# Sink-and-window attention with a highway layer on one core: later block loads in small rings, and the gate's bias split into eight pieces

## The chip, the cores and the metric

One core of a Trainium2 chip. The metric is device time in microseconds. The engines of the core run in order, each from its own queue, and wait for each other by semaphores: PE (matmul and weight load), DVE and ACT (elementwise work), POOL (GpSimd; it also issues the loads of q, k and v), and SP (it issues the stores).

## The reference

Attention with 4 batches, 8 heads, 768 positions and head size 64, in which each query sees the first 4 positions of its sequence (the sink) and the last 128; then a highway layer on the 3072 x 512 result.

```python
def _attn_ref(q, k, v, n_sink, window):
    scores = scale * np.matmul(q, k.transpose(0, 1, 3, 2))
    is_sink = pos[None, :] < int(n_sink)
    rel = pos[:, None] - pos[None, :]
    in_window = (rel >= 0) & (rel < int(window))
    scores = np.where(is_sink | in_window, scores, -1e9)
    a = np.exp(scores - np.max(scores, axis=-1, keepdims=True))
    a = a / (np.sum(a, axis=-1, keepdims=True) + 1e-09)
    return np.matmul(a, v)

def _moe_ref(x, w_h, w_t, b_t):
    H = np.maximum(x @ w_h, 0.0)
    T = 1.0 / (1.0 + np.exp(-(x @ w_t + b_t)))
    return T * H + (1.0 - T) * x
```

All inputs and the output are float32. The kernel computes in float16 with float32 accumulation, and writes the sigmoid as a tanh of half the argument.

## The kernel before, in words

The 3072 rows are 24 blocks of 128 queries, six to a batch. The keys and values of block n are loaded shifted by 64 positions (`chunk_parts`), so that a query block needs three pieces: its own shifted chunk n, half of chunk n+1, and half of chunk n-1. A shifted chunk at a batch border comes as two loads of 64 rows.

Each block passes through these steps, named as in the kernel's order string, with the engine and the line:

- `load_q`, `load_k`, `load_v` (POOL, L107, L114, L121): loads from DRAM that also convert to float16. q and k go to rotating buffers of a pool, v to the tiles of `v_ring`, in which a column of twos stands beside each head's 64 values for the row sums.
- `S` (PE): transposes of the q and k of a later block (L318; block n hosts those of block n+2), scores with the own chunk (`pe_SA`, L371) and with the two half chunks (`pe_SB`, L384; 64 x 64 matmuls on all four quarters of the array).
- `xx`, or `x0_` and `x1_` in early blocks (ACT, L398 and L393): the exponential, to the tile `e`. `tt`, or `tq` and `tk` (ACT, L330 and L323): the transposed q and k out of PSUM.
- `mm`, or `m0_` and `m1_` (DVE, L404): the mask. `sk` and `es` (PE L353, ACT L360): scores of the sinks and their exponential, for two blocks at a time after the first batch.
- `A` (PE): the values. `pe_AB` (L429) has 16 matmuls of 66 columns for the two half chunks, on the two quarters of the array that lead from one half of the rows to the other half of the columns; then eight full matmuls (L448) and two for the sinks (L454), all into the one PSUM tile `av`.
- `xh` (DVE, L462 and L467): division by the row sums. `X` (PE, L481) transposes the result into a spare part of `av`, and `xT` (ACT, or `xTV` on DVE, L486) copies it out; only then can the next `A` write `av`.
- `Mh` and `Mt` (PE, L509 and L497): the two products of the highway layer, into two PSUM banks `m`, which are dealt out by the string `M_BANKS` to these, to the sink scores and to the bias. The bias of `Mt` is a matmul of a row of ones by `bt16`: in blocks 0 to 7 one full matmul of 512 columns (L494), from block 9's `A` on (for the block before it) a pair of 64 x 64 matmuls of 512 columns in `pe_bias` (L437).
- `u` (ACT, L502), `U`, `d`, `e`, `o` (DVE, L521, L515, L526, L531): tanh, plus one, relu(H) minus x, product, sum; then the store by SP (L533).

The order on every engine is written out by hand in `ORDER`; a step issues its instructions in that order, so POOL's queue has the loads where the steps `A` stand: `do_A(n)` issues the loads of q of block n+8 and of k and v of chunk n+9. POOL itself does not wait for `A`; it waits only where a buffer is still read or the loads in flight hold it. At the first key chunk of batches 1 to 3, `new_T` puts the sinks' keys and values into block-diagonal tiles on POOL (`fill_ks`, L342, and `sink_v`, L181). The loads of the first blocks (q to 7, k and v to 8) are written out ahead of the loop.

Of the kernel before, what the change touches and what calls it, by code (L numbers as in the profile page):

```python
# [8 lines left out]
FP16 = mybir.dt.float16  # L9
# [11 lines left out]
def kernel(  # L21
# [18 lines left out]
    nc = tc.nc  # L40
    P = 128

    B, H, S, D = q.shape
# [8 lines left out]
    NSC = S // P  # L52
    assert NSC % 2 == 0
    NB = NT // P
# [4 lines left out]
    AHEAD = 8  # L59

    const = ctx.enter_context(tc.tile_pool(name="const", bufs=1))
    sd_pool = ctx.enter_context(tc.tile_pool(name="p_sd", bufs=AHEAD + 2))
    qkT_pool = ctx.enter_context(tc.tile_pool(name="p_qkT", bufs=7))
    tt_pool = ctx.enter_context(tc.tile_pool(name="p_tt", bufs=5))
    e_pool = ctx.enter_context(tc.tile_pool(name="p_e", bufs=3))
# [20 lines left out]

    ctx.callback(close_s)
    HP = P // 2
    B0 = 9
    M0 = 9  # L90
    NV = AHEAD + 5
    NS4 = H * NSINK
    KW = NHP * P + 32
    EW = P + HP
    v_ring = [const.tile([P, VW], FP16, tag=f"v{i}", name=f"v{i}") for i in range(NV)]
    q_sd, k_sd = {}, {}

    def chunk_parts(n):
        b, c = divmod(n, NSC)
        if c:  # L100
            return [(slice(0, P), b, c * P - HP)]
        return ([(slice(0, HP), b - 1, S - HP)] if b else []) + ([(slice(HP, P), b, 0)] if b < B else [])

    def load_q(n):
        b, c = divmod(n, NSC)
        qsd = sd_pool.tile([P, H, D], FP16, tag="qsd", name="qsd")
        nc.gpsimd.dma_start(out=qsd, in_=q[b, :, c * P:(c + 1) * P, :].transpose([1, 0, 2]))  # L107
        q_sd[n] = qsd

    def load_k(n):  # L110
        ksd = sd_pool.tile([P, H, D], FP16, tag="ksd", name="ksd")
        for rows, b, s0 in chunk_parts(n):
            nr = rows.stop - rows.start
            nc.gpsimd.dma_start(out=ksd[rows], in_=k[b, :, s0:s0 + nr, :].transpose([1, 0, 2]))  # L114
        k_sd[n] = ksd

    def load_v(n):
        vt = v_ring[n % NV][:, 0:H * 65].rearrange("p (h e) -> p h e", e=65)
        for rows, b, s0 in chunk_parts(n):
            nr = rows.stop - rows.start  # L120
            nc.gpsimd.dma_start(out=vt[rows, :, 0:D], in_=v[b, :, s0:s0 + nr, :].transpose([1, 0, 2]))  # L121
# [14 lines left out]
    bt32 = const.tile([P, DM], FP32, tag="bt32")  # L136
    bt16 = const.tile([P, DM], FP16, tag="bt16")
    ones_row = const.tile([P, P], FP16, tag="ones_row")
    ones2 = const.tile([P, P], FP16, tag="ones2")
    kf_first = const.tile([P, H, D], FP32, tag="kf0", name="kf0")  # L140
    ident32 = const.tile([P, P], FP32, tag="ident32")
    ident2 = const.tile([P, P], FP16, tag="ident2")
# [45 lines left out]
    with tc.manual_schedule(engines={ENG.Pool, ENG.SP}):  # L188
# [7 lines left out]
        for b in range(B):  # L196
            nc.sync.dma_start(out=vs_dn[b], in_=v[b, :, 0:NSINK, :])
        nc.gpsimd.affine_select(
            out=ident, in_=ident, compare_op=ALU.is_equal, fill=0.0,
# [14 lines left out]
            out=bm, in_=bm, compare_op=ALU.is_ge, fill=0.0,  # L214
            base=0, pattern=[[-NSINK, H]], channel_multiplier=1)
        nc.gpsimd.affine_select(
            out=bm, in_=bm, compare_op=ALU.is_ge, fill=0.0,
# [39 lines left out]
    def bias_rows(_):  # L257
        nc.vector.memset(bt16, 0.0)
        nc.vector.memset(ones_row, 0.0)
        nc.vector.memset(ones_row[0:1, :], 1.0)  # L260
        nc.vector.tensor_copy(out=ones2, in_=ones_row)
        nc.vector.memset(ones2[HP:HP + 1, :], 1.0)

    def bias_half(_):
        for r in (0, HP):
# [2 lines left out]
    def sink_ones(_):  # L268
# [3 lines left out]

    m_bank = [m_ps.tile([P, DM], FP32, tag=f"m{i}", name=f"m{i}") for i in range(2)]
    M_BANKS = (
        "010101010101010101010101010010100101001100101011010110101101"
    )
    m_next = iter(M_BANKS)

    def m_tile():
        return m_bank[int(next(m_next))]  # L280
# [7 lines left out]
    av_t, xh_of, xT_of, t_of, u_of, h_of, dd_of, ee_of, sk_of = {}, {}, {}, {}, {}, {}, {}, {}, {}  # L288
# [127 lines left out]
    def av_tile(n):  # L416
        if n not in av_of:
            av_of[n] = av_ps.tile([P, 2, 4, P], FP32, tag="av", name="av")
            av_t[n] = av_of[n]
        return av_of[n]  # L420

    def pe_AB(n):
        av = av_tile(n)
        nxt = v_ring[(n + 1) % NV]
        prv = v_ring[(n - 1 if n % NSC else n) % NV]
        lo, hi = slice(0, HP), slice(HP, P)
        for j in range(H):
            for src, part, vt, h in ((lo, hi, nxt, j), (hi, lo, prv, (j + 4) % H)):
                nc.tensor.matmul(  # L429
                    av[part, h // 4, h % 4, 0:_AVN], lhsT=e_at(n, h)[src, P:EW],  # L430
                    rhs=vt[src, 65 * h:65 * h + _AVN], start=(h % 4 == 0), stop=False,
                    skip_group_check=True)

    def pe_bias(n):
        t_of[n] = m_tile()
        for rows in (slice(0, HP), slice(HP, P)):
            nc.tensor.matmul(t_of[n][rows, :], lhsT=ones2[rows, rows], rhs=bt16[rows, :],  # L437
                             start=True, stop=False, skip_group_check=True)

    def pe_A(n):  # L440
        if n >= B0:
            pe_bias(n - 1)
        pe_AB(n)
        av = av_of[n]
        vt = v_ring[n % NV]
        b, c = divmod(n, NSC)
        for h in range(H):
            nc.tensor.matmul(  # L448
                av[:, h // 4, h % 4, 0:_AVN], lhsT=e_at(n, h)[:, 0:P],
                rhs=vt[:, 65 * h:65 * h + _AVN], start=False,  # L450
                stop=False, skip_group_check=True)
        if c:
            for g in range(2):
                nc.tensor.matmul(  # L454
                    av[:, g, :, 0:65], lhsT=es_of[n],
                    rhs=vs_bd[b % 2][:, 4 * g:4 * g + 4, :], start=False, stop=True,
                    skip_group_check=True)
        av_of[n] = av.rearrange("p g h e -> p (g h) e")
# [134 lines left out]
    def on(n):  # L593
        return 0 <= n < NB
# [33 lines left out]
            fill_ks(m // NSC, nc.gpsimd)  # L628
            sink_v(m // NSC, nc.gpsimd)

    def load_set(n):
        if on(n):
            load_q(n)
            load_k(n + 1)
            load_v(n + 1)

    def do_A(n):
        pe_A(n)
        load_set(n + AHEAD)

    def norm(n):
        dve_rec(n)
# [28 lines left out]
    }  # L671
    ORDER = """
    mz0_:0 ma:0 na:0 Tq:0 na:1 Tk:0 tq:0 mz1_:0 tk:0 ma:1 wA:0 wA:0 Tk:1 mc:0 cv:0 tk:1 fa:0
    wA:0 wA:0 wA:0 S:0 cv:1 x0_:0 fb:0 x1_:0 wA:0 wA:0 wA:0 wA:0 Tq:3 m0_:0 fc:0 tq:3 wA:0 Tk:2
    tk:2 m1_:0 fd:0 wA:0 wA:0 wA:0 wA:0 Tq:1 A:0 tq:1 S:1 xh:0 sk:1 x0_:1 x1_:1 Tq:2 m0_:1 X:0
    sk:3 xTV:0 es:1 Tk:3 m1_:1 tq:2 tk:3 wA:1 A:1 es:3 S:2 xh:1 x0_:2 x1_:2 Tk:4 m0_:2 sk:2
    tkV:4 X:1 es:2 m1_:2 S:3 xT:1 A:2 x0_:3 Mh:1 x1_:3 xh:2 tq:4 d:1 X:2 tk:5 Mh:0 xTV:2 m0_:3
    Mh:2 d:0 m1_:3 S:4 d:2 Mt:0 x0_:4 x1_:4 m0_:4 A:3 u:0 m1_:4 Mt:1 tq:5 xh:3 tk:6 U:0 sk:4 u:1
    e:0 S:5 es:4 o:0 X:3 x0_:5 U:1 sk:5 xTV:3 e:1 A:4 x1_:5 m0_:5 o:1 tq:6 Mt:2 xh:4 tk:7 es:5
    u:2 m1_:5 X:4 S:6 xT:4 U:2 e:2 A:5 x0_:6 o:2 Mh:3 x1_:6 xh:5 tq:7 Mh:4 m0_:6 tk:8 m1_:6 X:5  # L680
    d:3 S:7 xT:5 d:4 A:6 x0_:7 Mh:5 xh:6 x1_:7 Mt:3 d:5 tq:8 tk:9 m0_:7 X:6 u:3 m1_:7 Mt:5 xT:6
    U:3 e:3 sk:7 o:3 u:5 Tq:9 es:7 U:5 Mt:4 tq:9 e:5 o:5 S:8 u:4 U:4 A:7 x0_:8 e:4 o:4 Mt:6
    x1_:8 xh:7 tq:10 Mh:6 m0_:8 tk:10 m1_:8 u:6 X:7 d:6 S:9 xT:7 U:6 A:8 e:6 xx:9 o:6 sk:9 xh:8
    Mh:7 es:9 tt:9 mm:9 Mt:7 d:7 X:8 u:7 S:10 xTV:8 U:7 A:9 e:7 xx:10 o:7 Mt:8 xh:9 tt:10 Mh:8
    mm:10 u:8 X:9 d:8 S:11 xT:9 U:8 A:10 e:8 xx:11 o:8 sk:11 xh:10 Mt:9 es:11 tt:11 mm:11 Mh:9
    u:9 X:10 d:9 S:12 xT:10 U:9 A:11 e:9 xx:12 o:9 Mt:10 xh:11 tt:12 Mh:10 mm:12 u:10 X:11 d:10
    S:13 xT:11 U:10 A:12 e:10 xx:13 o:10 sk:13 xh:12 Mt:11 es:13 tt:13 mm:13 Mh:11 u:11 X:12
    d:11 S:14 xT:12 U:11 A:13 e:11 xx:14 o:11 Mh:12 xh:13 tt:14 Mt:12 mm:14 X:13 d:12 u:12 S:15
    xT:13 U:12 e:12 xx:15 A:14 o:12 sk:15 xh:14 Mt:13 tt:15 mm:15 es:15 X:14 S:16 u:13 xTV:14
    U:13 A:15 xx:16 Mh:14 xh:15 tt:16 Mt:14 d:14 mm:16 Mh:13 u:14 U:14 sk:17 d:13 X:15 es:17  # L690
    S:17 xT:15 e:13 e:14 A:16 xx:17 o:13 o:14 Mt:15 xh:16 tt:17 Mh:15 mm:17 u:15 X:16 S:18 d:15
    xT:16 U:15 A:17 xx:18 e:15 o:15 Mh:16 xh:17 tt:18 Mt:16 mm:18 X:17 u:16 S:19 xTV:17 d:16
    A:18 xx:19 U:16 e:16 sk:19 xh:18 Mt:17 es:19 mm:19 tt:19 Mh:17 o:16 u:17 X:18 S:20 d:17
    xT:18 U:17 A:19 xx:20 e:17 o:17 Mh:18 xh:19 tt:20 Mt:18 mm:20 X:19 u:18 S:21 xTV:19 d:18
    A:20 xx:21 U:18 e:18 sk:21 o:18 Mt:19 es:21 xh:20 tt:21 Mh:19 mm:21 u:19 X:20 S:22 d:19
    xT:20 U:19 A:21 xx:22 e:19 o:19 Mh:20 xh:21 tk:24 Mt:20 mm:22 X:21 u:20 S:23 xTV:21 d:20
    A:22 xx:23 U:20 e:20 sk:23 xh:22 Mt:21 es:23 mm:23 X:22 u:21 Mh:21 xT:22 o:20 A:23 d:21 U:21
    Mt:22 xh:23 e:21 X:23 u:22 Mh:22 xTV:23 o:21 Ta:23 d:22 Ha:23 ua:23 U:22 e:22 Tb:23 da:23
    o:22 Hb:23 ub:23 db:23 ea:23 eb:23 pa:23 pb:23
    """  # L700

    with tc.manual_schedule(engines={ENG.PE, ENG.DVE, ENG.Activation, ENG.SP, ENG.Pool}):
        warm_up(8)
        identities(0)
        for step in ORDER.split():
            op, n = step.split(":")
# [36 lines left out]
```

## Time and profile before

| | us |
|---|---|
| median of three runs | 124.76 |
| the three runs | 126.43, 121.55, 124.76 |
| the profiled execution | 121.67 |
| its span, first to last instruction | 119.5 |
| PE busy | 107.5 (90%) |
| DVE busy | 105.0 (88%) |
| ACT busy | 87.8 (73%) |
| POOL busy | 72.6 (61%) |
| granted TensorE clock, mean | 0.987 |

"PE" rows are matmuls and "PEld" rows weight loads, which overlap. Strings of 40 digits give the busy share of 40 equal slices of the span (3.0 us each) in tenths; 9 is 90% or more. In lists of waits a line gives the waiting engine and line, what it waited for, the total in us, the number of times and the longest. In timelines a line gives start and length in us, engine, line, operation, tiles and count. POOL's load instruction lasts as long as its issue; the landing comes later.

### The profile page before, as it was taken

The numbers are of one execution on the slowest core, as the hardware profiler recorded it, in microseconds if no ns is written. First come the engines' busy times: TensorE is split into PE (matmuls) and PEld (weight loads), VectorE is DVE, ScalarE is ACT, GpSimd is POOL, SyncE is SP. The second block draws the span as 40 slices with busy tenths as digits, with TensorE's granted clock in tenths as the row PEclk, the third lists the DMA queues.
The fourth block names the chain that finished last, engine by engine and source line by source line (L and its number), as shares of the span: only waits on it lengthen the run. The fifth ranks groups of instructions, "written<-read, shape, count | busy, mean of one in ns | idle before, by whom it ended". The sixth has DMA issues, their size and how long they took to land.

```text
span 119.5 us, 4971 instructions
## 1 busy us (share of the span) xinstructions
PE 107.5 (90%) x2119; PEld 65.5 (55%) x2119; DVE 105.0 (88%) x252; ACT 87.8 (73%) x123; POOL 72.6 (61%) x97
## 2 busy tenths in 40 slices
PE   5998676999899999799998999999999999999920
PEld 1443454655765546556754665657556665565610
DVE  6889666596999899999999999969999999999990
ACT  2248196929998978788898999987998979773210
POOL 5999886959799799967779999986000000000000
PEclk9999999999999999999999999999999999999995
DMA  2999999999999999999999999999920222011132
GB/s 55 217 172 153 146 180 174 194 153 151 128 194 209 207 137 183 191 205 205 177 195 219 118 198 157 205 203 157 207 84 12 89 92 93 26 67 73 52 139 88
DMA packets 79848, 17.64 MB, mean 148 GB/s; under 512 B 75602, under 2 KB 76882, under 8 KB 79828
## 3 DMA queue, kind: packets, MB, share of 16 engines
q0 software_dynamic: 71888, 9.97, 134.2%
q1 hardware_dynamic: 6884, 7.12, 19.2%
q10 hardware_dynamic: 1056, 0.26, 1.3%
q8 instruction: 16, 0.26, 0.9%
q14 instruction: 4, 0.03, 0.1%
HBM read 21.01 MB, written 6.29 MB: 228 GB/s over the span
## 4 chain that ended last, share of the span: by engine, by line
PE 63%; DVE 16%; DMA 7%; ACT 4%; issue 3%; POOL 3%; DVEq 0%; ACTq 0%
PE m L509 15%; PE m L497 11%; DMA qsd<-in_q_dram 7%; PE av L448 6%; PE av L429 6%; PE sps L384 4%; PE sps L318 4%; PE sps L371 4%; PE av L481 4%; DVE xh L467 4%; DVE otok L531 3%; PE av L454 3%; ACT e L393 3%; PE m L353 2%; DVE e L404 2%
## 5 line engine op out<-in xcount | busy, mean ns | idle before, releaser
L404 DVE TENSOR_TENSOR e<-e,mask 128x768 f16<-128x768 f16 (+1 forms) x33 | 24.8, 758 | 2.4 <-ACT e L393 2.3
L398 ACT ACTIVATE e<-sps,ebias 128x1536 f16<-128x1536 f32 x15 | 23.1, 1542 | 3.2 <-PE sps L384 3.0
L121 POOL DMA_DIRECT2D v<-in_v_dram x26 | 22.2, 854 | 4.7 <-DVE t L323 1.0
L509 PE MATMUL m<-wh_sb,xT 128*128 128x512 f16 x92 | 23.5, 379 | 0.3 <-issue 0.3
L497 PE MATMUL m<-wt_sb,xT 128*128 128x512 f16 x92 | 23.6, 379 | 0.0
L114 POOL DMA_DIRECT2D ksd<-in_k_dram x26 | 22.3, 861 | 2.0 <-DMA v<-in_v_dram 1.8
L107 POOL DMA_DIRECT2D qsd<-in_q_dram x23 | 21.2, 924 | 1.0 <-DMA qsd<-in_q_dram 0.5
L393 ACT ACTIVATE e<-sps,ebias 128x768 f16<-128x768 f32 x18 | 15.3, 898 | 5.3 <-PE sps L384 4.8
L502 ACT ACTIVATE u<-m 128x512 f16<-128x512 f32 x23 | 13.7, 597 | 6.5 <-PE m L497 6.3
L467 DVE TENSOR_TENSOR xh<-av,rec 128x512 f16<-128x512 f32 x24 | 16.6, 691 | 0.8
L531 DVE SCALAR_TENSOR_TENSOR otok<-xh,ee 128x512 f32<-128x512 f16 x23 | 15.8, 688 | 0.6
L515 DVE SCALAR_TENSOR_TENSOR dd<-m,xh 128x512 f16<-128x512 f32 x23 | 15.7, 686 | 0.1
L509 PEld LDWEIGHTS <-xT 128*128 128x128 f16 x92 | 8.6, 98 | 9.1 <-issue 1.0
L497 PEld LDWEIGHTS <-xT 128*128 128x128 f16 x92 | 8.8, 98 | 8.0
L330 ACT COPY tt<-sps 128x1024 f16<-128x1024 f16 x13 | 13.0, 999 | 0.0
L323 ACT COPY t<-sps 128x512 f16<-128x512 f16 x19 | 10.4, 590 | 2.1 <-PE sps L318 2.1
L429 PEld LDWEIGHTS <-e 64*64 64x64 f16 x384 | 9.9, 107 | 2.7 <-issue 1.9
L429 PE MATMUL av<-v,e 64*64 64x66 f16 x384 | 10.8, 193 | 0.4 <-DVE xT L486 0.3
L448 PE MATMUL av<-v,e 128*128 128x66 f16 x192 | 10.4, 195 | 0.0
L526 DVE TENSOR_TENSOR ee<-u,dd 128x512 f16<-128x512 f16 x23 | 9.7, 427 | 0.7
L486 ACT COPY xT<-av 128x512 f16<-128x512 f16 x15 | 8.7, 581 | 1.7 <-PE av L481 1.6
L481 PEld LDWEIGHTS <-xh 64*128 64x128 f16 x192 | 4.2, 95 | 10.2 <-DVE xh L467 7.4
(94 smaller groups left out, 173.5 us busy)
## 6 DMA issues: line engine op xcount, KB each, us to landing
out_dram<-otok SPq DMA_DIRECT2D x23, 256.0 KB, 4.7
qsd<-in_q_dram POOLq DMA_DIRECT2D x23, 128.0 KB, 7.2
ksd<-in_k_dram POOLq DMA_DIRECT2D x19, 128.0 KB, 7.1
v<-in_v_dram POOLq DMA_DIRECT2D x19, 128.0 KB, 7.1
wh_sb<-in_moe_w_h_dram POOLq DMA_DIRECT2D x1, 512.0 KB, 7.9
wt_sb<-in_moe_w_t_dram POOLq DMA_DIRECT2D x1, 512.0 KB, 8.4
ksd<-in_k_dram POOLq DMA_DIRECT2D x7, 64.0 KB, 6.9
v<-in_v_dram POOLq DMA_DIRECT2D x7, 64.0 KB, 6.3
```

Source lines behind the costliest of these rows:

```text
L107: nc.gpsimd.dma_start(out=qsd, in_=q[b, :, c * P:(c + 1) * P, :].transpose([1, 0, 2]))
L114: nc.gpsimd.dma_start(out=ksd[rows], in_=k[b, :, s0:s0 + nr, :].transpose([1, 0, 2]))
L121: nc.gpsimd.dma_start(out=vt[rows, :, 0:D], in_=v[b, :, s0:s0 + nr, :].transpose([1, 0, 2]))
L393: nc.scalar.activation(out=e_tile(n)[:, g].rearrange("p a b c -> p a (b c)"), in_=s_tile(n, g)[:, :, 0:2 * EW], func=AF.Exp, bias=ebias, s ...
L398: nc.scalar.activation(out=e_tile(n).rearrange("p g a b c -> p (g a) (b c)"), in_=s_of[n][:, :, 0:2 * EW], func=AF.Exp, bias=ebias, scale= ...
L404: nc.vector.tensor_tensor(out=ev, in0=ev, in1=m.unsqueeze(1).to_broadcast([P, k, EW]), op=ALU.mult)
L429: nc.tensor.matmul(av[part, h // 4, h % 4, 0:_AVN], lhsT=e_at(n, h)[src, P:EW], rhs=vt[src, 65 * h:65 * h + _AVN], start=(h % 4 == 0), sto ...
L448: nc.tensor.matmul(av[:, h // 4, h % 4, 0:_AVN], lhsT=e_at(n, h)[:, 0:P], rhs=vt[:, 65 * h:65 * h + _AVN], start=False, stop=False, skip_g ...
L467: nc.vector.tensor_tensor(out=xh.rearrange("p (h d) -> p h d", d=D), in0=av_of.pop(n)[:, :, 0:D], in1=rec_of.pop(n).unsqueeze(2).to_broadc ...
L497: nc.tensor.matmul(t_of[n], lhsT=xT[:, kc, :], rhs=wt_sb[:, kc, :], start=False, stop=(kc == NOC - 1), skip_group_check=True)
L509: nc.tensor.matmul(hps, lhsT=xT[:, kc, :], rhs=wh_sb[:, kc, :], start=(kc == 0), stop=(kc == NOC - 1))
L531: nc.vector.scalar_tensor_tensor(out=otok, in0=xh_of.pop(n), scalar=2.0, in1=ee_of.pop(n), op0=ALU.mult, op1=ALU.add)
```

## The change

Three things change together.

First, the loads. q and k of blocks up to 8 keep a pool (now of eight buffers, before ten); from block 9 on they come from a pool with three buffers each. v of chunks 0 to 8 have a tile each, and those from 9 on rotate through five tiles. `do_A(n)` issues the loads of v of chunk n+4, of q of block n+6 and of k of chunk n+6.

Second, the bias of the gate. `pe_bias` is gone; `pe_AB` itself issues, after each of its eight pairs of value matmuls, a pair of 64 x 64 matmuls of 64 columns on the two other quarters of the array. It does so for blocks 1, 2, 3 and 6 to 22, as `T_BESIDE` says (a key is the `A`, its value the block whose bias it carries); blocks 0, 4 and 5 keep the full matmul in `pe_Mt`. The second tile of ones is dropped.

Third, the written order. `xT` of blocks 19, 21 and 23 goes from DVE to ACT and that of block 4 from ACT to DVE; the copy of q3 goes to DVE; one more spare matmul stands early; a few DVE steps trade places (among them `d` of block 3, now ahead of block 6's masks, and `o` of block 2, now behind `d` of block 4). `M_BANKS` has a new string. The order of the other steps on PE is the same.

```diff
-    sd_pool = ctx.enter_context(tc.tile_pool(name="p_sd", bufs=AHEAD + 2))
+    late_pool = ctx.enter_context(tc.tile_pool(name="p_late", bufs=3))
+    sd_pool = ctx.enter_context(tc.tile_pool(name="p_sd", bufs=AHEAD))
...
-    B0 = 9
+    T_BESIDE = {3: 1, 4: 2, 6: 3, 7: 6, 8: 7, 9: 8, 10: 9, 11: 10, 12: 11, 13: 12, 14: 13, 15: 14, 16: 15, 17: 16, 18: 17, 19: 18, 20: 19, 21: 20, 22: 21, 23: 22}
     M0 = 9
-    NV = AHEAD + 5
+    FIRST = 9
+    NV = FIRST + 5
...
+    def vi(n):
+        return n if n < FIRST else FIRST + (n - FIRST) % (NV - FIRST)
...
-        qsd = sd_pool.tile([P, H, D], FP16, tag="qsd", name="qsd")
+        qsd = (sd_pool if n < FIRST else late_pool).tile([P, H, D], FP16, tag="qsd", name="qsd")
...
-        nc.vector.memset(ones_row[0:1, :], 1.0)
-        nc.vector.tensor_copy(out=ones2, in_=ones_row)
-        nc.vector.memset(ones2[HP:HP + 1, :], 1.0)
+        nc.vector.memset(ones_row[0:1, 0:HP], 1.0)
+        nc.vector.memset(ones_row[HP:HP + 1, HP:P], 1.0)
...
     def pe_AB(n):
         av = av_tile(n)
-        nxt = v_ring[(n + 1) % NV]
-        prv = v_ring[(n - 1 if n % NSC else n) % NV]
+        nxt = v_ring[vi(n + 1)]
+        prv = v_ring[vi(n - 1 if n % NSC else n)]
         lo, hi = slice(0, HP), slice(HP, P)
+        m = T_BESIDE.get(n)
+        if m is not None:
+            t_of[m] = m_tile()
         for j in range(H):
             for src, part, vt, h in ((lo, hi, nxt, j), (hi, lo, prv, (j + 4) % H)):
                 nc.tensor.matmul(
                     av[part, h // 4, h % 4, 0:_AVN], lhsT=e_at(n, h)[src, P:EW],
                     rhs=vt[src, 65 * h:65 * h + _AVN], start=(h % 4 == 0), stop=False,
                     skip_group_check=True)
-
-    def pe_bias(n):
-        t_of[n] = m_tile()
-        for rows in (slice(0, HP), slice(HP, P)):
-            nc.tensor.matmul(t_of[n][rows, :], lhsT=ones2[rows, rows], rhs=bt16[rows, :],
-                             start=True, stop=False, skip_group_check=True)
+            if m is not None:
+                cols = slice(D * j, D * j + D)
+                for part in (lo, hi):
+                    nc.tensor.matmul(
+                        t_of[m][part, cols], lhsT=ones_row[part, part], rhs=bt16[part, cols],
+                        start=(j == 0), stop=False, skip_group_check=True)
...
-    def load_set(n):
-        if on(n):
-            load_q(n)
-            load_k(n + 1)
-            load_v(n + 1)
-
     def do_A(n):
         pe_A(n)
-        load_set(n + AHEAD)
+        if FIRST <= n + 4 <= NB:
+            load_v(n + 4)
+        if AHEAD <= n + 6 < NB:
+            load_q(n + 6)
+        if FIRST <= n + 6 <= NB:
+            load_k(n + 6)
```

More of the change, by code (lines that the diff above doesn't have):

```diff
@@ L110, in load_k @@
     def load_k(n):
-        ksd = sd_pool.tile([P, H, D], FP16, tag="ksd", name="ksd")
+        ksd = (sd_pool if n < FIRST else late_pool).tile([P, H, D], FP16, tag="ksd", name="ksd")
         for rows, b, s0 in chunk_parts(n):
@@ L117, in load_v @@
     def load_v(n):
-        vt = v_ring[n % NV][:, 0:H * 65].rearrange("p (h e) -> p h e", e=65)
+        vt = v_ring[vi(n)][:, 0:H * 65].rearrange("p (h e) -> p h e", e=65)
         for rows, b, s0 in chunk_parts(n):
@@ L138 @@
     ones_row = const.tile([P, P], FP16, tag="ones_row")
-    ones2 = const.tile([P, P], FP16, tag="ones2")
     kf_first = const.tile([P, H, D], FP32, tag="kf0", name="kf0")
@@ L274 @@
     M_BANKS = (
-        "010101010101010101010101010010100101001100101011010110101101"
+        "010101010101010010101000101101011010110011010100101001010010"
     )
@@ L432, in pe_AB @@
                     skip_group_check=True)
-    def pe_bias(n):
-        t_of[n] = m_tile()
-        for rows in (slice(0, HP), slice(HP, P)):
-            nc.tensor.matmul(t_of[n][rows, :], lhsT=ones2[rows, rows], rhs=bt16[rows, :],
-                             start=True, stop=False, skip_group_check=True)
+            if m is not None:
[4 more added lines that the diff above has]
+                        start=(j == 0), stop=False, skip_group_check=True)
     def pe_A(n):
-        if n >= B0:
-            pe_bias(n - 1)
         pe_AB(n)
         av = av_of[n]
-        vt = v_ring[n % NV]
+        vt = v_ring[vi(n)]
         b, c = divmod(n, NSC)
@@ L673 @@
     mz0_:0 ma:0 na:0 Tq:0 na:1 Tk:0 tq:0 mz1_:0 tk:0 ma:1 wA:0 wA:0 Tk:1 mc:0 cv:0 tk:1 fa:0
-    wA:0 wA:0 wA:0 S:0 cv:1 x0_:0 fb:0 x1_:0 wA:0 wA:0 wA:0 wA:0 Tq:3 m0_:0 fc:0 tq:3 wA:0 Tk:2
-    tk:2 m1_:0 fd:0 wA:0 wA:0 wA:0 wA:0 Tq:1 A:0 tq:1 S:1 xh:0 sk:1 x0_:1 x1_:1 Tq:2 m0_:1 X:0
-    sk:3 xTV:0 es:1 Tk:3 m1_:1 tq:2 tk:3 wA:1 A:1 es:3 S:2 xh:1 x0_:2 x1_:2 Tk:4 m0_:2 sk:2
+    wA:0 wA:0 wA:0 S:0 fb:0 x0_:0 cv:1 x1_:0 wA:0 wA:0 wA:0 wA:0 Tq:3 tqV:3 m0_:0 wA:0 Tk:2 tk:2
+    m1_:0 fc:0 wA:0 wA:0 wA:0 wA:0 wA:0 Tq:1 fd:0 A:0 tq:1 S:1 xh:0 sk:1 x0_:1 x1_:1 Tq:2 m0_:1
@@ L677 @@
+    X:0 sk:3 xTV:0 es:1 Tk:3 m1_:1 tq:2 tk:3 wA:1 A:1 es:3 S:2 xh:1 x0_:2 x1_:2 Tk:4 m0_:2 sk:2
     tkV:4 X:1 es:2 m1_:2 S:3 xT:1 A:2 x0_:3 Mh:1 x1_:3 xh:2 tq:4 d:1 X:2 tk:5 Mh:0 xTV:2 m0_:3
[L678 to L699, printed above, removed]
+    Mh:2 d:0 m1_:3 S:4 d:2 Mt:0 x0_:4 x1_:4 m0_:4 A:3 u:0 m1_:4 tq:5 Mt:1 xh:3 tk:6 sk:4 U:0 u:1
@@ new lines @@
+    e:0 S:5 es:4 o:0 X:3 x0_:5 sk:5 xTV:3 U:1 A:4 x1_:5 m0_:5 e:1 tq:6 Mt:2 xh:4 tk:7 es:5 m1_:5
+    X:4 u:2 S:6 xTV:4 o:1 A:5 x0_:6 U:2 e:2 Mh:3 x1_:6 xh:5 tq:7 Mh:4 d:3 tk:8 m0_:6 X:5 S:7
+    xT:5 m1_:6 d:4 A:6 x0_:7 o:2 Mh:5 x1_:7 xh:6 Mt:3 tq:8 d:5 tk:9 X:6 m0_:7 u:3 Mt:5 m1_:7
+    xT:6 U:3 e:3 sk:7 u:5 o:3 Tq:9 es:7 Mt:4 tq:9 U:5 e:5 o:5 S:8 u:4 A:7 U:4 x0_:8 e:4 o:4
+    x1_:8 Mt:6 xh:7 tq:10 Mh:6 tk:10 m0_:8 u:6 m1_:8 X:7 S:9 d:6 xT:7 U:6 A:8 xx:9 e:6 o:6 sk:9
+    xh:8 es:9 tt:9 Mh:7 mm:9 Mt:7 d:7 X:8 u:7 S:10 xTV:8 U:7 A:9 xx:10 e:7 o:7 Mt:8 xh:9 tt:10
@@ new lines @@
+    Mh:8 mm:10 u:8 X:9 d:8 S:11 xT:9 U:8 A:10 xx:11 e:8 o:8 sk:11 Mt:9 xh:10 es:11 tt:11 Mh:9
+    mm:11 u:9 X:10 d:9 S:12 xT:10 U:9 A:11 xx:12 e:9 o:9 Mt:10 xh:11 tt:12 Mh:10 mm:12 u:10 X:11
+    d:10 S:13 xT:11 U:10 A:12 xx:13 e:10 o:10 sk:13 Mt:11 xh:12 es:13 tt:13 Mh:11 mm:13 u:11
+    X:12 d:11 S:14 xT:12 U:11 A:13 xx:14 e:11 o:11 Mh:12 xh:13 tt:14 Mt:12 mm:14 X:13 u:12 d:12
+    S:15 xT:13 U:12 e:12 xx:15 A:14 o:12 sk:15 xh:14 Mt:13 tt:15 mm:15 es:15 X:14 S:16 u:13
+    xTV:14 U:13 xx:16 A:15 Mh:14 xh:15 tt:16 Mt:14 d:14 mm:16 Mh:13 u:14 U:14 sk:17 d:13 X:15
@@ new lines @@
+    es:17 S:17 xT:15 e:13 e:14 A:16 xx:17 o:13 o:14 Mt:15 tt:17 xh:16 Mh:15 u:15 mm:17 X:16 S:18
+    xT:16 d:15 A:17 U:15 xx:18 e:15 o:15 Mh:16 xh:17 tt:18 Mt:16 mm:18 X:17 u:16 S:19 xTV:17
+    d:16 A:18 xx:19 U:16 sk:19 xh:18 Mt:17 es:19 mm:19 tt:19 Mh:17 e:16 u:17 X:18 o:16 S:20
+    xT:18 d:17 A:19 xx:20 U:17 e:17 Mh:18 o:17 tt:20 xh:19 Mt:18 mm:20 X:19 u:18 S:21 xT:19 d:18
+    xx:21 A:20 U:18 e:18 o:18 sk:21 Mt:19 tt:21 xh:20 es:21 mm:21 u:19 Mh:19 U:19 X:20 d:19 S:22
+    xT:20 e:19 xx:22 A:21 o:19 Mh:20 xh:21 tk:24 Mt:20 mm:22 X:21 d:20 u:20 S:23 xT:21 U:20 e:20
@@ L700 @@
+    xx:23 A:22 o:20 sk:23 xh:22 Mt:21 es:23 mm:23 X:22 u:21 Mh:21 xT:22 U:21 A:23 d:21 e:21
+    Mt:22 xh:23 o:21 u:22 X:23 Mh:22 xT:23 U:22 Ta:23 d:22 Ha:23 ua:23 e:22 Tb:23 da:23 o:22
+    Hb:23 ub:23 ea:23 db:23 eb:23 pa:23 pb:23
     """
```

## The prediction

> **What bounds the kernel now.** I read the engine shares first, then the waits from 54 us on, the chain of waits, the windows by stage, and the timelines around the two places that the change touches. The engine shares say that two engines are full:
>
> ```profile
> span 119.5 us, 4971 instructions
> PE 107.5 (90%) x2119; PEld 65.5 (55%) x2119; DVE 105.0 (88%) x252; ACT 87.8 (73%) x123; POOL 72.6 (61%) x97
> PE   5998676999899999799998999999999999999920
> DVE  6889666596999899999999999969999999999990
> POOL 5999886959799799967779999986000000000000
> DMA  2999999999999999999999999999920222011132
> ```
>
> DVE is full from slice 10 on. POOL is a third engine that looks full, and so are the transfers, but both stop at slice 28 or 30 of 40: every load has been issued at 80 us, while the compute goes on for 39 us. Loads run ahead of use, so neither sets the steady pace. The waits after 54 us name who does:
>
> ```profile
> PEld L481 <- DVE xh L467: 4.4, 10, 0.5
> ACT u L502 <- PE m L497: 3.2, 7, 0.8
> ACT e L398 <- PE sps L384: 2.8, 11, 0.4
> DVE rec L462 <- PE av L454: 0.9, 1, 0.9
> ```
>
> PE waits ten times, 0.44 us each, for DVE's `xh`; DVE waits for PE's value matmuls once. So DVE sets the pace there and PE has about 0.4 us of slack in a block. No load appears. One block of DVE is L404 0.948 + L462 0.20 + L467 0.69 + L515 0.685 + L521 0.28 + L526 0.425 + L531 0.69 = 3.92 us, less four overlaps of 0.08 us plus three gaps of 0.034 us = 3.70 us, and 0.34 us more (0.417 less an overlap) where DVE also copies `xT`. The blocks of the trace come every 3.69 to 4.12 us. Before 13.4 us the chain is the landing of the third q load (13.35 us); nothing in the change touches that.
>
> **The loads.** All 75 block loads stay, in the same order up to v of block 7; only when a later one may start changes. Before, q and k have ten buffers and POOL runs on until loads in flight hold it (issue 0.87 us apart, landing about 7 us). After, q and k from block 9 on have three buffers each, v five. So q(n) waits for the transposes of q(n-3) in S(n-5), v(n-2) ahead of it in POOL's queue waits for A(n-6), and k(n) follows. The three issues take 3 x 0.88 = 2.65 us after A(n-6). Need is S(n-2), three blocks later less one S (0.7 us) and one A (1.0 us): in the trace A(10) ends at 59.42 and the k transposes of S(14) start at 69.80, 10.4 us. From the end of an issue to its landing the trace has 2.9 us (after POOL's pause at 42.5), 3.4 us (after the one at 64.7), 5 to 6 us in the run that follows, and 8.1 us at the worst (49.5 us, three outputs and a full queue). With at most three loads queued I take the rows after a pause, 3.4 to 3.9: k lands 2.65 + 3.9 = 6.6 us after A, 3.8 us early. By 8.1 it would be 0.35 us late. So the transfers cost nothing by the near row; the cover is 3.8 us. Queued behind a waiting load are only the next loads and the sink work of a batch (L342, L181, 1.8 us); the first of these (`ks`, `vs` of batch 1) moves ahead of 9 loads, from 40.7 to about 30.7 us; those of batches 2 and 3 wait for ACT's `tt` copies (56.98 and 80.35 us in the trace), which end before the next A does, so no load is late behind them.
>
> What moves is POOL's interference with DVE:
>
> ```profile
> 40.71 0.46 POOL L342 COPY ks<-t 64x16 f16<-64x16 f16 x2
> 41.25 1.29 POOL L181 TENSOR_TENSOR vs<-vd,bm 32x512 f16<-32x512 f32 x1
> 42.50 0.94 POOL L107 DMA_DIRECT2D qsd<-in_q_dram  x1
> ```
>
> ```profile
> 41.10 1.86 DVE L404 TENSOR_TENSOR e<-e,mask 128x768 f16<-128x768 f16 x2
> 42.88 0.65 DVE L521 TENSOR_SCALAR u<-u 128x512 f16<-128x512 f16 x1
> ...
> 44.63 0.68 DVE L521 TENSOR_SCALAR u<-u 128x512 f16<-128x512 f16 x1
> ```
>
> One L404 took 1.39 us under POOL's L181, where its like take 0.55: 0.84 lost. L521 takes 0.282 us with POOL idle (nine of 23) and 0.28 to 0.77 beside load issues; its excess over all 23 is 2.35 us. These stand on the chain of waits, where DVE is the path from 40 to 49 us. After, POOL issues q8, q9, k9 from 28.0 us, does the sink work till 32.5, issues six more loads (6 x 0.87) till 37.7, and rests until the q9 transposes (43.3 us). Then L404's 0.84 goes, unless L181 meets another mask at 31 us; of three L181 one did such harm, so I take 2/3 of 0.84 = 0.56. Of L521 the one at 42.88 is freed (0.37), those at 44.6 and 46.4 meet the q12 and k12 issues, and later ones start 2.8 us after an A, just as the three issues end: I take 0.5 of the 2.35, bounds -2 (new collisions to 98 us, where POOL was idle) and +2.35. [...]
>
> **The bias in pieces.** Two 64x64 matmuls of 512 columns (L437) ahead of the 16 value matmuls (L429) become 16 of 64 columns among them; from block 9 on 15 x 14 matmuls and weight loads more.
>
> ```profile
> 61.98 0.32 PE L384 MATMUL sps<-tt 64*64 64x64 f16 x16
> 62.12 0.39 PE L437 MATMUL m<-bt,ones 64*64 64x512 f16 x2
> 62.27 0.45 PE L429 MATMUL av<-v,e 64*64 64x66 f16 x16
> 62.65 0.43 PE L448 MATMUL av<-v,e 128*128 128x66 f16 x8
> ```
>
> L384 is the model: 16 matmuls of 64 columns that use all four quarters of the array. Their starts come in fours, 3 ns apart, 32 ns from four to four (53 for the first), 126 ns in all. L429 uses two quarters: pairs, 32 ns apart, 255 ns. A pair plus a bias pair is again a four of 32 ns, so the stretch stays 255 ns; bounds 255 to 511 (fours that go as two pairs). What is removed is worth nothing from block 9 on: L429 starts 0.165 us after L384, when ACT's `xT` copy frees `av` (62.22 us), and L437 lies in that wait. If no overlap came, 0.26 us a block on PE would still lie in its 0.4 us of slack, save about 0.1 in blocks with a sink matmul. [...]
>
> Blocks 1, 2, 3, 6 and 7 lose a full bias matmul (L494, 0.216 us): 1.08 us of PE in a stage where DVE was busy 17.2 of 18 us. I take 0.2, bounds 0 and 1.08.
>
> **The reordered copies.** `xT` of blocks 19 and 21 goes from DVE to ACT: 2 x 0.34 = 0.67 off the pacing engine. ACT then carries 1.54 + 1.0 + 0.6 + 0.58 and up to 0.45, less overlaps, 3.4 to 3.75 us a block, as much as DVE, so I take 0.6. Block 23's copy lies beside Mh(22) and gives 0. `xT` of block 4 comes to DVE: -0.34. The output of block 2 moves behind the d of block 4, into a DVE gap of 0.37 us at 39.3: +0.35. q3's copy goes to DVE before 14 us, where q1's landing is the path: 0. The dropped `ones2` lies there too.
>
> **Sum.** 0.56 + 0.5 + 0.2 + 0.6 - 0.34 + 0.35 = 1.9 us. The profiled execution took 121.67 us, span 119.5 and 2.2 around it; the sum gives 117.6 and 119.8 us. That execution and the fastest of the three runs (121.55) agree; the other two were 3 and 5 us longer, the median 3.09 over it. I move the forecast up by three tenths of that, 0.9, to 120.7, for the chance that its median falls among longer runs. Its own range: 118.5 to 123.
>
> **Rivals.**
> 1. More is freed: every L521 excess (2.35), L404 whole (0.84), all of L494 (1.08), 0.6 from the copies: 4.9 us, time 116.8. For it: these lie on a full DVE. Against: POOL's work is the same and now lasts till 98 us, and once DVE is quicker PE, with 0.4 us to spare, takes over. Chance 0.17.
> 2. A late k takes the place of the free prefetch: the ring of three ties POOL to PE. If landing takes 8.1 us, issue to need is 2.65 + 8.1 + 1.7 = 12.45 us for three blocks, 4.15 a block where A(9) to A(23) now take 3.88 each; 12 blocks x 0.27 = 3.3, with nothing gained 125.0 us. It decides from 7.75 us of landing on (10.4 less 2.65); rows after pauses (3.4) speak against, the three outputs at 44 to 48 us for. Beside it on the same side: bias fours that go as pairs and meet sinks, some 1 to 3 us. Chance together 0.20: slower.
> 3. The change does not do what it says: loads were early and stay early, the bias was hidden and stays so, collisions come back elsewhere. 121.7 us. Chance 0.15.
> The forecast has 0.48, half of it beyond 2% by its spread of terms (2% of 121.67 is 2.4 us; 2% is about what a measurement of this kernel can tell from no change).
>
> **How the numbers follow.** Faster by over 2%: 0.24 + 0.17 = 0.41; within: 0.24 + 0.15 = 0.39; slower: 0.20. The range runs from rival 1's neighbourhood to just past rival 2, 117.0 to 125.5, and leaves out about 0.08 below and 0.1 above.
>
> **What would show it.** Right: load issues in groups of three until about 98 us and a POOL gap near 38 to 43 us; no PE wait for q or k after 14 us; 16 value and 16 bias matmuls starting within 0.27 us; `xT` of 19 and 21 on ACT without a new wait. Wrong: waits of L321 (after's transposes) for q or k, a value stretch near 0.5 us, more L521 over 0.4 us than the six now.

## The result, and the profile after

Slower. The changed kernel takes 126.8 us in the median of four runs (125.53 to 129.83), the kernel before 123.16 in the same comparison; the ratio is 1.041, 95% interval 1.029 to 1.053. The ratios with intervals leave out runs over 1.5% longer than the fastest of the same kernel; the medians keep all runs. The forecast was 120.7 us in a range of 117.0 to 125.5. The profiled execution is the longest of the four (129.83 us, span 127.8), so its total is not set against the forecast; what it shows in kind recurs in the experiments.

The engine shares, the 40 slices and the instruction queue, from the page of the changed kernel:

```profile
span 127.8 us, 5549 instructions
PE 107.9 (84%) x2405; PEld 65.2 (51%) x2405; DVE 104.8 (82%) x252; ACT 88.2 (69%) x124; POOL 72.3 (57%) x97
DVE  6889645969998979889999987078996998899880
POOL 6999986698960199669589457842792130000000
PEclk9999999999999999999999999869999999999997
DMA  3999999999999199999999999990999794012222
q8 instruction: 19, 0.31, 1.0%
```

DVE has as much to do as before (104.8 us now, 105.0 before) and PE too (107.9 and 107.5), though PE has 286 matmuls more. Yet DVE is not full any more: slices 26 and 27, counted from 1, show 0 and 7, and many show 8. POOL's pause is where it was forecast (no load issue from 37.3 to 44.3 us), and its last load issue is at 102.7 us, where about 98 was forecast. The engines have the same work as before and wait more. The waits of the changed kernel, over its whole span, say for what; a line gives the waiting engine and line, what it waited for, the total in us, the number of times and the longest:

```profile
PEld L513 <- issue: 4.0, 7, 1.6
PEld L435 <- issue: 3.0, 8, 0.7
PEld L452 <- issue: 2.7, 2, 2.0
PE av L452 <- issue: 2.6, 2, 1.9
PE m L442 <- issue: 2.1, 3, 0.9
DVE rec L466 <- PE av L458: 7.5, 6, 3.3
ACT u L506 <- PE m L501: 11.9, 12, 3.8
```

"issue" means that the engine waited for nothing that the profile shows. DVE and ACT wait for PE, and in the PE lines here no semaphore and no data is named. In the list of before, from 54 us on, the same kind stands with less weight:

```profile
PEld L509 <- issue: 1.0, 3, 0.6
PEld L429 <- issue: 0.9, 4, 0.3
```

No load is late: after 13 us no wait of PE for q, k or v is in the list. Nor do the pieces take array time. The PE timeline of a stall (start, length, engine, line, operation, tiles, count, idle before):

```profile
75.27 0.20 PE L442 MATMUL m<-bt,ones_row 64*64 64x64 f16 x2
75.27 0.22 PE L435 MATMUL av<-v,e 64*64 64x66 f16 x2
76.38 0.22 PE L442 MATMUL m<-bt,ones_row 64*64 64x64 f16 x2 [0.89 <-issue]
76.39 0.22 PE L435 MATMUL av<-v,e 64*64 64x66 f16 x2
```

Here PE stops in the middle of the value matmuls of block 14, for 1.08 us from start to start. Below, a stall is a gap of over 0.6 us between two PE starts that the profile puts down to "issue". In 17 of the 20 stretches with pieces nothing of the kind happens, and their 32 matmuls start within 255 to 269 ns, like the 16 of before (255 in the median).

What ends these stalls is found among the transfer packets. The queue called "instruction" (q8) brings 16 KB packets; the page counts it, like the loads, on the core's 16 transfer engines. There are 16 packets for 4238 recorded matmuls and weight loads before, 19 for 4810 after, so about 265 and 253 to a packet. Against the packets' landings, the stalls of the changed kernel stand so:

```
packet landed (us)   29.28  36.12  53.91  58.68  74.98  80.64  94.43  99.75
PE goes on (us)      30.93  37.68  55.27  60.04  76.38  82.12  96.04 101.20
stall (us)            1.06   1.44   0.75   0.76   1.08   2.09   1.05   0.80
```

Each ends 1.35 to 1.66 us after a landing. The kernel before has two, 0.98 us (ends at 19.74) and 0.69 us (64.92), 1.44 and 1.89 us after a landing. That is eight stalls against two, and 9.0 us against 1.7, though the profile of before is of one of its shorter runs. The twelve profiles of this study have 30 such stalls, and all end 1.30 to 1.90 us after a landing, while packets land 5.8 us apart in the mean of the changed kernel and 5.9 before; each also ends before the last load of its run has landed.

The places of the stalls in PE's program say the same. Count all PE records of a trace in order of start (matmuls, weight loads and PE's semaphore instructions). Ahead of the instruction with which PE goes on stand 449, 961, 1217, 1985, 2241, 2497, 2753, 3009, 3265, 3777 or 4033 records, in all 30 stalls and in every version of the kernel. Each of these counts is 193 more than a multiple of 256. In the two profiles of before and after the multiple is the number of packets landed by then: 961 is 193 + 3 x 256, and PE goes on there after the third landing; 4033 is 193 + 15 x 256, after the fifteenth. The other places of this kind agree: PE reaches each of the 18 in the changed kernel and each of the 15 in before with just that many packets landed, the last of them at least 1.35 us earlier. So by this count a packet holds 256 of PE's instructions, and PE stops only where one packet's end and the next packet's begin: it has run out of instructions.

The longest stall of this profile costs twice. In windows of the changed kernel (window, length, then busy us of PE, PEld, DVE, ACT and POOL with counts, then the granted PE clock, the transfer share and GB/s):

```profile
78.00:82.00 4.00, 2.23 (x87) 1.42 (x85) 1.72 (x4) 3.19 (x4) 3.17 (x4) 0.98 1.58 150
82.00:85.20 3.20, 3.08 (x13) 1.45 (x13) 1.35 (x3) 0.15 (x1) 2.39 (x5) 0.50 1.84 121
85.20:88.00 2.80, 2.80 (x67) 1.66 (x68) 2.44 (x6) 1.42 (x3) 0.00 (x0) 0.99 0.20 12
```

With the stall of 2.09 us the granted clock is halved for 3.413 us (from 81.82 us): 13 matmuls in 3.2 us, 0.43 us for each of 512 columns where 0.216 is usual.

### The profile page after: what moved, and what is told of

The parts are those of the page before. It is cut to its first block, busy times and chain, and to the rows that moved or that the text cites. A ratio compares the mean times of both kernels' runs of the same rounds, so it can differ in the third digit from the quotient of the medians.

```text
span 127.8 us, 5549 instructions
## 1 busy us (share of the span) xinstructions
PE 107.9 (84%) x2405; PEld 65.2 (51%) x2405; DVE 104.8 (82%) x252; ACT 88.2 (69%) x124; POOL 72.3 (57%) x97
## 4 chain that ended last, share of the span: by engine, by line
PE 58%; issue 11%; ACT 9%; DVE 9%; DMA 6%; POOL 3%; DVEq 0%; ACTq 0%
PE m L513 16%; PE m L501 11%; DMA qsd<-in_q_dram 6%; PE av L452 5%; PE av L435 4%; PE sps L321 4%; ACT e L396 4%; PE sps L387 3%; PE av L485 3%; PE sps L374 3%; PE av L458 3%; DVE xh L471 2%; ACT xT L490 2%; PE m L442 2%; PE m L356 2%
## 5 line engine op out<-in xcount | busy, mean ns | idle before, releaser
L513 PE MATMUL m<-wh_sb,xT 128*128 128x512 f16 x92 | 24.4, 390 | 2.0 <-issue 1.1
L466 DVE RECIPROCAL rec<-av 128x8 f32<-128x8 f32 x24 | 4.9, 204 | 9.8 <-PE av L458 7.5
L435 PE MATMUL av<-v,e 64*64 64x66 f16 x384 | 11.3, 194 | 1.3 <-ACT xT L490 1.1
L490 ACT COPY xT<-av 128x512 f16<-128x512 f16 x17 | 9.9, 582 | 3.0 <-PE av L485 3.0
L326 ACT COPY t<-sps 128x512 f16<-128x512 f16 x18 | 9.8, 590 | 2.0 <-PE sps L321 2.0
L442 PE MATMUL m<-bt,ones_row 64*64 64x64 f16 x320 | 9.3, 195 | 2.1 <-issue 2.1
```

Source lines behind the costliest of these rows:

```text
L435: nc.tensor.matmul(av[part, h // 4, h % 4, 0:_AVN], lhsT=e_at(n, h)[src, P:EW], rhs=vt[src, 65 * h:65 * h + _AVN], start=(h % 4 == 0), sto ...
L513: nc.tensor.matmul(hps, lhsT=xT[:, kc, :], rhs=wh_sb[:, kc, :], start=(kc == 0), stop=(kc == NOC - 1))
```

## The experiments

Theory I: PE runs out of instructions. More of them in the same time need packets more often, and a packet is late when it queues behind load packets. Theory II: the small rings crowd the transfers for longer and so delay the packets. Rival III: the pieces themselves cost, by array time or clock. Times are medians of the runs of one comparison; "before" beside them is the kernel before on the same chip in the same comparison. Runs e1 to e4 share a comparison and came without an interval; the kernel before took 120.57 to 125.78 us in its seven runs there, and its median lies 1.8 us over that of the comparison above, from which the changed kernel's 126.8 us come. Differences between the two comparisons are therefore good to about 2 us.

**The bias as a pair again, all else as changed (e1).**

```diff
+        if m is not None:
+            for part in (lo, hi):
+                nc.tensor.matmul(
+                    t_of[m][part, :], lhsT=ones_row[part, part], rhs=bt16[part, :],
+                    start=True, stop=False, skip_group_check=True)
         for j in range(H):
...
-            if m is not None:
-                cols = slice(D * j, D * j + D)
-                ...
```

> The changed kernel with one edit: the 16 bias matmuls of 64 columns become a pair of 512 columns ahead of the value matmuls, in the same blocks (280 matmuls and as many weight loads fewer). Theory I, PE's instruction supply (each 16 KB packet of the instruction queue holds 256 instructions; in the changed kernel eight PE stalls of 0.75 to 2.1 us end 1.35 to 1.65 us after such a packet landed): about two stalls over 0.6 us are left, and the time falls to 119 to 122 us. Theory II, the small rings (loads last until 107 us instead of 86 and crowd the transfer engines that also carry the instructions): stalls stay at six or more and the time at 125 to 127 us.

Measured: 122.04 us (120.87 to 122.91), before 124.94; 4.8 us less than the changed kernel. The profiled execution has no stall over 0.6 us. This speaks for theory I and against theory II.

**The old loads, the bias in pieces (e2).**

```diff
-        if FIRST <= n + 4 <= NB:
-            load_v(n + 4)
-        if AHEAD <= n + 6 < NB:
-            load_q(n + 6)
-        if FIRST <= n + 6 <= NB:
-            load_k(n + 6)
+        if on(n + AHEAD):
+            load_q(n + AHEAD)
+            load_k(n + AHEAD + 1)
+            load_v(n + AHEAD + 1)
```

with ten buffers for q and k and thirteen for v.

> The changed kernel with the loads of before (ten buffers for q and k, thirteen for v, eight to nine blocks ahead); the bias stays in pieces. Theory I (instruction supply): stalls stay at six or more, 125 to 127 us. Theory II (small rings): two stalls or so, 120 to 122 us.

Measured: 131.6 us (130.72 to 134.07), before 124.94. Worse than the changed kernel by 4.8 us: theory II has the wrong sign, and theory I's figure was too low. The profile has six stalls, 8.0 us in sum, the longest 1.96 us, and two stretches of half clock, at 79.1 and 86.0 us.

**Old loads and pairs, so that the order alone is new (e3).** Both edits above at once.

> The changed kernel with both edits undone at once: loads of before and the bias as pairs, so that only the written order, the banks and the blocks that get their bias beside the value matmuls differ from the kernel before. Theory I and II alike: 119 to 122 us, and against the kernel with pairs alone it tells what the rings are worth: equal within 1 us by theory I, 4 us quicker by theory II.

Measured: 124.78 us (123.35 to 126.59), before 124.94, where 119 to 122 were expected. The new order shows no gain. The rings are worth 2.7 us with pairs (e1 beside this run) and 4.8 us with pieces (the changed kernel beside e2); "equal within 1 us" was wrong. The profile has three stalls, of 1.24, 1.57 and 1.52 us, and e1's, with as many PE instructions, has none. So with the old loads packets come late even without the pieces; with the rings they come late less often.

**Pieces in the kernel before (e4).**

```diff
-            pe_bias(n - 1)
...
+            if n >= B0:
+                cols = slice(D * j, D * j + D)
+                for part in (lo, hi):
+                    nc.tensor.matmul(
+                        t_of[n - 1][part, cols], lhsT=ones2[part, part], rhs=bt16[part, cols],
+                        start=(j == 0), stop=False, skip_group_check=True)
```

> The kernel before with one edit: from block 9 on the pair of 512-column bias matmuls becomes 16 of 64 columns among the value matmuls (210 matmuls and weight loads more). Theory I (instruction supply): five or more PE stalls from 54 us on, 124 to 127 us against 122 to 124 for the kernel before. Theory II (small rings): as the kernel before within 1 us, two stalls.

Measured: 127.64 us (126.02 to 129.33), before 124.94, 2.7 us more. After 54 us the profile has stalls of 1.95 us (ends at 63.5) and 2.50 us (82.2) where five were expected: fewer, longer ones, with half clock from 63.7 us. The last blocks, which have no stall, speak against rival III: from `xh` of block 17 to `xh` of block 23 this kernel takes 21.94 us and the kernel before as long, though 83 more matmuls and as many more weight loads are recorded there.

**The instructions without the work (e5).**

```diff
+            if n >= B0 and j < H - 1:
+                for part in (lo, hi):
+                    nc.tensor.matmul(
+                        t_of[n - 1][part, 0:2], lhsT=ones2[part, part], rhs=bt16[part, 0:2],
+                        start=True, stop=True, skip_group_check=True)
+        if n >= B0:
+            pe_bias(n - 1)
...
     def pe_A(n):
-        if n >= B0:
-            pe_bias(n - 1)
```

The edit also moves the bias pair from ahead of the value matmuls to behind them.

> The kernel before, with 14 matmuls of 2 columns added among the value matmuls of each block from block 9 on (the bias pair of 512 columns overwrites what they wrote): as many PE instructions as the kernel before with pieces, and next to no more work in the array. Theory I (the count of PE instructions): as that kernel, 126 to 129 us, with stalls that end 1.3 to 1.9 us after an instruction packet landed. Rival III (the pieces' own columns, by array time or by the clock they draw): as the kernel before within 1 us.

Measured: 126.03 us, before 123.21; ratio 1.030 (1.020 to 1.039). With matmuls of two columns the kernel is slowed as much as with those of 64 (1.022 by e4's medians). Not all of it is the count: from `xh` of block 17 to that of block 23, where no stall lies, this run takes 22.75 us, 0.8 more than before and e4, presumably for the moved pair. The rest of the loss is stalls, which the instructions bring though they have next to no columns. Rival III falls by this run and e4 together. Three lines of its waits, in the form of the lists above:

```profile
PEld L437 <- issue: 2.7, 1, 2.7
PE m L437 <- issue: 2.6, 1, 2.6
PEld L384 <- issue: 1.7, 2, 0.9
```

One stall alone, ahead of the bias pair at 64.3 us, is 2.75 us long from start to start; another, at 80.5 us, is 1.02 us.

**The changed kernel without the later loads (e6).**

```diff
-        if FIRST <= n + 4 <= NB:
-            load_v(n + 4)
-        if AHEAD <= n + 6 < NB:
-            load_q(n + 6)
+        if n + 6 == AHEAD:
+            load_q(n + 6)
+        if AHEAD < n + 6 < NB:
+            q_sd[n + 6] = q_keep[0]
         if FIRST <= n + 6 <= NB:
-            load_k(n + 6)
+            k_sd[n + 6] = k_keep[0]
```

and every v tile from 9 on is tile 8.

> The changed kernel without the loads of q from block 9 and of k and v from chunk 9 on; later blocks read the last loaded tiles instead, so that the values differ from the reference's. PE's instructions are those of the changed kernel. Theory I in the form that instruction packets wait behind load packets: no stall over 0.6 us after 45 us, and 118 to 120 us. Theory I in the form that the count alone is too much for the instruction queue: six stalls stay, 124 to 127 us.

Measured: 121.36 us (121.02 to 122.09 over ten runs), before 123.21; ratio 0.991 (0.986 to 0.996). PE's program is that of the changed kernel, 19 packets. From its page and its waits:

```profile
span 119.6 us, 5447 instructions
POOL 5999985958300000002300000060000000000000
DMA  2999999999922224022022220202220402220222
q8 instruction: 19, 0.31, 1.1%
...
PEld L359 <- issue: 1.4, 1, 1.4
```

The transfers are busy up to slice 11 and much less after it, and with them the long stalls end: the only one, 1.52 us, ends at 31.4 us, while the first loads still run. So the count alone is not too much; it takes the loads in the transfer queues. The time was expected at 118 to 120 us, and why it stays above that is open: e10, which has no pieces, takes 121.17 us. That these two agree within 0.2 us says that the pieces cost next to nothing once the later loads are gone.

This run also narrows down where a late packet loses its time, since its PE program is that of the changed kernel. Take the instruction that PE had reached when a packet began in e6. In the changed kernel the packets of seven of the eight stalls begin 1.6 to 2.7 us after PE has reached that instruction. Six of these seven then take 0.89 to 1.07 us for the transfer and one 1.83, where e6's packets take 0.88 to 1.48. So most of the delay lies ahead of the packet's own transfer. (The eighth, at 30.93 us, begins where it does in e6, and that run stalls there too.)

**The rings alone on the kernel before (e7).**

```diff
-        load_set(n + AHEAD)
+        if FIRST <= n + 4 <= NB:
+            load_v(n + 4)
+        if AHEAD <= n + 6 < NB:
+            load_q(n + 6)
+        if FIRST <= n + 6 <= NB:
+            load_k(n + 6)
```

with the pools and `vi` of the changed kernel.

> The kernel before with the new loads alone (three buffers for q and k and five for v from block 9 on). Theory I: fewer load packets are queued when an instruction packet is asked for, so at most one stall, 120 to 122 us against 123 to 125 for the kernel before. Theory II (rings crowd the transfers to 100 us): three stalls or more, over 125 us. Were the written order of the changed kernel worth something, this one would lie over the 122.0 us of the kernel with rings and pairs.

Measured: 121.35 us (119.57 to 123.62), before 123.21; ratio 0.983 (0.978 to 0.989). It is faster than both kernels (by 1.7% against the kernel before) and the version to keep. From its page:

```profile
span 118.8 us, 4975 instructions
POOL 5999984949799039976959628887794220000000
DMA  2999999999999959999999999999899996012132
q8 instruction: 16, 0.26, 0.9%
```

The profile has one stall over 0.6 us, 1.30 us long (before: two, 1.7 us). POOL is busy to slice 33 here, with load issues until 95.0 us, and that is no loss.

**Four pieces of 128 columns (e8).**

```diff
-            if m is not None:
-                cols = slice(D * j, D * j + D)
+            if m is not None and j % 2 == 0:
+                cols = slice(D * j, D * j + 2 * D)
```

> The changed kernel with the bias in four pieces of 128 columns instead of eight of 64: 240 matmuls and weight loads more than with pairs, where the changed kernel has 560 more. Theory I (count): between the 122.0 us of pairs and the 126.8 us of the changed kernel, 123 to 125 us, with two to five stalls. Rival III (short columns): as with pairs, 121 to 123 us.

Measured: 123.42 us, before 123.21; ratio 1.010 (1.004 to 1.015), two stalls, 1.7 us. The number of pieces counts: with the rings and the new order the ratio to the kernel before is 0.994 for pairs (e9, below), 1.010 for four pieces and 1.041 for eight.

**The kernel before without the later loads (e10).** The edit of e6 in the kernel before.

> The kernel before without the loads of q from block 9 on and of k and v from chunk 9 on; later blocks read the last loaded tiles, so that the values differ from the reference's. If instruction packets that wait behind load packets are what spreads the kernel's times (121.2 to 127.3 us over 25 runs), the spread shrinks to about 1 us with no stall after 45 us, and the median falls to 119 to 121 us. If the spread is the chip's own, it stays several us.

Measured: 121.17 us (120.73 to 122.77, four runs), before 123.23 (121.56 to 125.89, 17 runs); ratio 0.989 (0.981 to 0.998), one stall, 0.71 us at 19.1. The median just misses the 119 to 121 us expected. The spread falls to 2.0 us over four runs, and in e6 to 1.1 us over ten, so most of it goes with the loads; one run of the four still lay 1.4 us over the others.

**Rings and pairs again, over more runs (e9).** The kernel of e1.

> The kernel with the new loads, the new written order and the bias as pairs, once more and in more rounds, to compare it with the kernel before by an interval. Theory I: as the rings alone, a ratio of 0.975 to 0.99. If the new order is worth what the forecast gave it (about 0.6 us), it lies 0.5% under the rings alone (0.983).

Measured: 121.78 us (120.99 to 122.78, 12 runs), before 123.23; ratio 0.994 (0.990 to 0.999). The rings alone have 0.983 in another comparison; by the medians of all runs the two are closer, 0.988 here and 0.985 there. So the new order, which here comes with the bias of blocks 1, 2, 3, 6 and 7 beside the values, shows no gain.

The traces show why: the order gains early and loses late. The starts of `xh`, in us:

```
run                       order   block 8   block 17   block 23   17 to 23
e7 (rings alone)          old       50.50      87.58     109.51      21.93
e10 (no later loads)      old       51.28      87.22     109.15      21.93
e9 (rings and pairs)      new       49.81      86.39     109.49      23.10
e6 (no later loads)       new       50.27      86.66     109.74      23.08
```

Up to block 8 the new order is 0.7 to 1.0 us ahead. From block 17 to block 23, where three `xT` copies have gone to ACT, it loses 1.15 us. The kernel before and e4 have 21.94 us there, e1 and e2 23.10 and 23.16; the other three kernels with the new order take 23.6 us or more. Which of its parts costs was not tried.

## Why the prediction was wrong, point by point

- **The bias in pieces, term 0: the step that failed.** "The stretch stays 255 ns" held (255 to 269 ns in 17 of 20): the time is not lost in these stretches. But the bounds, 255 to 511 ns, priced the pieces as array work alone. The 14 extra matmuls and 14 weight loads of a block were counted, and then given no cost as instructions to be brought in. From block 9 on a block has about 88 matmuls and 88 weight loads before, 102 and 102 after: at 3.9 us a block a packet of 256 lasts, by estimate from these counts, 5.7 us before and 4.9 us after. With the loads in the queues the next packet is then too late more often (eight stalls against two). The term, put at 0, measured 4.8 us of loss with the rings (e1 to the changed kernel), 2.7 us on the kernel before (e4), and next to nothing without the later loads (e6 beside e10).
- **The row that said so was on the page.** The waits of before had PE "issue" lines, 1.0 us on L509 among them, which lay in the very list that the prediction quoted from, and the quotation left them out. The prediction does not mention them, and none of its signs of being wrong looks for them: no load was late, the stretch stayed at 255 ns, and only three plus-ones took over 0.4 us, where before had six.
- **PE's 0.4 us of slack** did not cover this: a late packet stops PE for 0.75 to 2.1 us at a time in the changed kernel (2.75 in e5), not 0.1 us in each block, and then DVE runs dry (its waits for L458, 7.5 us).
- **The loads, term 0: right.** No load was late. From 44 us on k landed 3.6 to 6.6 us after the end of its issue; the prediction took 3.9, so the cover was thinner than its 3.8 us, but all lie under the 7.75 at which rival 2 decides. Rival 2 forecast the right side by a mechanism that did not occur.
- **The interference of POOL with DVE, 0.56 + 0.5: right in sign, wrong in place.** In the rings alone a mask lost 0.10 us at most (0.65 us at 33.21) and the excess of plus-one (L521 before) fell from 2.35 to 0.99 us. In the changed kernel POOL's sink work, now at 31.0 us, met another mask (1.39 us at 31.06), the one in three that the term allowed for; the plus-one's excess was 1.71. The rings' whole gain, 1.7% or about 2 us, is near the 1.06 forecast, but part of it comes from fewer late instruction packets, which the forecast did not have; the runs do not split the two.
- **The written order, 0.2 + 0.6 - 0.34 + 0.35: not found in sum.** The times are 124.78 against 124.94 us (e3). Its early part came true in kind (0.7 to 1.0 us by block 8, in e9 and e6). The 0.6 for the copies of blocks 19 and 21 has the wrong sign: the blocks from 17 to 23 take 1.15 us longer. Nor is the pace of 3.69 to 4.12 us a block what the trace of before has: `xh` comes 3.27 to 5.33 us apart from block 9 on.
- **The allowance of 0.9 us** read the spread of the runs as chance. It is largely a matter of how often an instruction packet comes late: without the later loads it falls to 1.1 us over ten runs (e6) and 2.0 us over four (e10).

What stays open: that loads must be in the queues is shown, and that most of a late packet's delay lies ahead of its transfer; whether it waits behind loads at one transfer engine or is asked for too late is not. Which part of the order costs the 1.15 us late in the run is open too.

## What to carry to other kernels

Count PE's instructions as transfers too (here 16 packets of 16 KB before, 19 after), and read the "issue" waits of PE as a resource: small matmuls that fill idle quarters of the array within the same 255 ns can still cost by their instructions, here 4.8 us with the loads in flight (e1 to the changed kernel) and next to nothing without the later loads (121.36 us in e6, 121.17 in e10). Before splitting a matmul, look for stalls that end soon after an instruction packet lands (here 1.30 to 1.90 us) and stand a fixed number of instructions apart (here multiples of 256), and test with matmuls of two columns, which here brought stalls of 2.75 and 1.02 us with next to no columns (e5). Keeping fewer loads in flight can pay even where no load was late: the rings alone gave 1.7% (e7).

## What the runs showed of the hardware

- The queue called "instruction" brought 16 packets of 16 KB for 4238 recorded matmuls and weight loads before, 19 for 4810 after; in both profiles PE reached record 193 + 256 n with n of them landed, the last at least 1.35 us earlier. In all 30 stalls over 0.6 us PE stopped at a multiple of 256 instructions plus 193, and went on 1.30 to 1.90 us after a landing.
- With four PE stalls of 1.55 to 2.09 us (two in e2, one each in the changed kernel and e4) the granted clock was 0.5 for 3.41 us. With others of 1.52 to 1.58 us (e2, e3, e6), of 2.50 us (e4) and of 2.75 us (e5) it was not, so the length of a stall alone does not decide.
- Sixteen 64-column matmuls on two quarters and sixteen of 66 columns on the two others started within 255 to 269 ns in 17 of the changed kernel's 20 stretches, as the sixteen of 66 columns did alone before (255 ns in the median).
- Beside POOL's tensor operation on the sinks a DVE mask took 1.39 us where 0.55 is usual (before, at 41.56 us; changed kernel, at 31.06), and a plus-one 1.04 us (changed kernel, at 58.65) or 1.05 us (e7, at 56.7) where 0.28 is usual.
